# One chunk's state exchange of an mLSTM and MoE kernel: the same product on GpSimd, both states in one bank

## The chip, the cores and the metric

The kernel runs on one core of a Trainium2 chip. The metric is the device time of one execution in microseconds (us). The core has a matmul engine (TensorE, PE in the profile, with its weight loads as PEld), VectorE (DVE), ScalarE (ACT), GpSimd (POOL) and a queue for transfers (SyncE, SP). The engines run side by side and wait for each other by semaphores. PSUM, in which matmuls leave their results, has eight banks.

## The reference

Three stages follow one another. The first is a recurrent attention over 2 batches, 8 heads, 768 steps and 40 columns a head, with a decaying state `C` for each head:

```
for t in range(S):
    m_new  = maximum(f_gate[t] + m, i_gate[t])
    C      = exp(f_gate[t] + m - m_new) * C + exp(i_gate[t] - m_new) * outer(v[t], k[t])
    n      = exp(f_gate[t] + m - m_new) * n + exp(i_gate[t] - m_new) * k[t]
    y[t]   = sigmoid(o_gate[t]) * (C @ q[t]) / maximum(abs(n @ q[t]), 1)
x = y as 1536 tokens x 320
x = (h - tanh(h)) @ w_out,        h = x @ w_in      # layer 1, 2048 columns of h
x = (h * tanh(softplus(h))) @ w_out, h = x @ w_in   # layer 2, weights of its own
```

## The kernel before

The attention is computed in 6 chunks of 128 steps (c = 0 to 5). A tile is one chunk of one batch, 128 tokens with all 8 heads; the 12 tiles are numbered j = 2c + b, so that both batches of a chunk follow each other. Inside a tile, `sc` (L406) holds the scores of its steps among each other, `Dm` the weights from the gates, with a causal mask laid over it on GpSimd (L383); L410 multiplies both in place in `Dm`. `it` (L417) is what the state `C` of all chunks before gives, `pv` (L430) what the tile's own steps give. The sum is normed (L434 to L444: `hv`, `den`, `xo`) and, as the tokens `xo`, transposed on TensorE (`xt`, L296) into `xT` for layer 1. `xT` is kept as a rounded part, written by ScalarE (L298), and a low part that VectorE subtracts (L302, L304), because matmuls take a rounded 32-bit form (fp32r) and products are split into a high and a low part.

At the end of a tile the state is carried on. This is the exchange. `dl` (L171, called from L393) copies the last column of `Dm` into a small tile, `wv` (L394) multiplies the values of the tile by it, 8 small matmuls (`states`, L322; the trace counts each of such 32-bit matmuls as two) make of `wv` and the keys what the tile adds to the state, in a bank `st` of PSUM. Then `C` is multiplied by a decay `dec` of the chunk and `st` is added. For chunks 2 and later this is done for both batches at once, after the first batch's tile: 16 matmuls into one bank, one decay pass over `C` of both batches (L476), two sums (L479), all on VectorE. For chunk 1 each batch does it by itself, with 8 matmuls and a bank of its own, four decay passes on GpSimd in all (L459) and four sums on VectorE (L461). Chunk 0 copies.

Layer 1 runs in blocks of two tiles, 256 tokens. Its 16 slices of 128 columns go in pairs: h (L606, 8 matmuls a slice), then the function of h in steps on ScalarE and VectorE (L628 to L637), then its rounded part `gh` on ScalarE (L617) and its low part `gl` on GpSimd (L618), then `acc` (L669 to L671). The slices of a block are begun while the next tiles' attention runs, so TensorE has work of both. Weights come raw in a packed form and are unpacked in passes on VectorE and ScalarE (L204, L212, L216, L219, L222). Layer 2 begins at about 257 us and has blocks of 512 tokens.

The order of instructions on each engine is decided when the kernel is built, by a scheduler that works from its own estimate of how long each operation takes, under the data's dependences and a few edges `after(...)` written into the code. Work further down the program can therefore change places when an operation changes. From the second block on, the attention's PSUM tiles (`xt`, `st`, `nb`, `sc`, `it`, `pv`) share three banks in turn, so each of them waits until the one three before it is read. `nb` (L371) makes the gate terms of a half of `Dm`, which ScalarE reads through its exponential (L375); only chunks 0 to 2 have it.

For tile 2 (`j == NP`) an edge makes the copy `dl` wait for `rests[1]`, the `gl` of layer 1's second step, so that the copy comes behind that `gl` on GpSimd.

Of the kernel before, what the change touches and what calls it, by code (L numbers as in the profile page):

```python
# [12 lines left out]
ALU = mybir.AluOpType  # L13
# [12 lines left out]
def kernel(  # L26
# [11 lines left out]
    nc = tc.nc  # L38
    B, P, _, HG, S = qk.shape
    H, L = 2 * HG, 128  # L40
# [3 lines left out]
    D = DM // H  # L44
    NF, _, WC = w1.shape
    D1 = D + 1
# [17 lines left out]
    def cut(sizes, p0=0):  # L64
        r = []
        for n in sizes:
            r.append(list(range(p0, p0 + n)))
            p0 += n
        return r

    blocks1 = cut(BLOCKS)
    flat = cut([n for s in SUPER for n in s])
# [53 lines left out]
    dec = once.tile([P, B, HG, NCH], F32, name="dec")  # L126
# [4 lines left out]
    last, chain, fill, mark, second = [], [], [], [], []  # L131

    texp, tbl, dls, squared = [], [], [], []
# [14 lines left out]
    def after(x):  # L148
        e = ExitStack()
        for i in x:  # L150
            e.enter_context(tc.issue_after(i.ins))
        return e
# [12 lines left out]
    def copy_r(eng, o, x):  # L165
        if eng == 0:
            nc.scalar.activation(out=o, in_=x, func=AF.Copy)
        elif eng == 1:
            nc.vector.tensor_copy(o, x)
        else:  # L170
            nc.gpsimd.tensor_scalar(o, in0=x, scalar1=1.0, scalar2=0.0, op0=ALU.mult, op1=ALU.add)  # L171
# [103 lines left out]
    def at_ps(shape, name):  # L275
        p, tag = at_pools[0]
        if len(at_pools) > 1:
            at_pools.append(at_pools.pop(0))
        return p.tile(shape, F32, tag=tag, name=name)
# [37 lines left out]
    def states(st, k, wv, first):  # L317
        with in_turn(first=first) as turn:
            for g in range(HG):
                for r in range(2):  # L320
                    h = HG * r + g
                    turn(lambda: nc.tensor.matmul(  # L322
                        st[HP * r:HP * r + D, g, :], lhsT=k[:, h, :], rhs=wv[:, h, :], start=True, stop=True
                    ))
        return turned[-1:]
# [5 lines left out]
    def attention(j):  # L331
        b, c = order[j]
# [16 lines left out]
        Dm = att.pop(("D", j)) if c >= RC else ap_.tile([P, H, L], F32, tag="D", name="Dm", bufs=2)  # L349
        for hf in range(2):  # L350
            if c < RC:
                nb = at_ps([P, HG, L], "nb")
                flat = nb.rearrange("p g s -> p (g s)")
            if c < EC:
                bh = b * H + HG * hf
                nc.tensor.matmul(
                    flat, lhsT=na[c], rhs=sel[:, bh:bh + HG].rearrange("p (g o) -> p g o", o=1).to_broadcast([P, HG, L]),
# [30 lines left out]
        C = Cst[b]  # L388
        if c + 1 < NCH:
            wv = ap_.tile([P, H, D1], F32, tag="wv", name="wv", bufs=2)  # L390
            dl = ap_.tile([P, H, 1], F32, tag="dl", name="dl")
            with after([rests[1]] if j == NP else []):
                copy_r(2, dl, Dm[:, :, L - 1:L])  # L393
            dls[:] = [nc.gpsimd.tensor_tensor(wv, in0=v, in1=dl.to_broadcast([P, H, D1]), op=ALU.mult)]  # L394
            if c > 1:
                news.append((k, wv))
        scs = [at_ps([P, HG, L], "sc") for _ in range(2)]
        held = []
# [15 lines left out]
        if c > 0:  # L414
            it = at_ps([P, HG, 2, D1], "it")
            for g in range(HG):
# [7 lines left out]
                in1=u.to_broadcast([P, 2, HG, D1]), op=ALU.mult,  # L424
# [10 lines left out]
        else:  # L435
# [9 lines left out]
            x, in0=x, scalar=1 / WS, in1=den.to_broadcast([P, H, D]), op0=ALU.mult, op1=ALU.mult  # L445
# [3 lines left out]
        copy_r(0, xo[:, j, DM:3 * P], xo[:, j, 2 * P:DM])  # L449
        yield "x"  # L450
        if c + 1 < NCH:
            if c < 2:
                st = at_ps([P, HG, D1], "st")
                states(st, k, wv, chain[:1])
                for r in range(2):
                    sl = slice(HP * r, HP * r + D)
                    if c:
                        dc = dec[sl, b, :, c:c + 1].to_broadcast([D, HG, D1])
                        nc.gpsimd.tensor_tensor(C[sl, :, r, :], in0=C[sl, :, r, :], in1=dc, op=ALU.mult)  # L459
                        with after(chain[2:]):  # L460
                            nc.vector.tensor_tensor(C[sl, :, r, :], in0=C[sl, :, r, :], in1=st[sl], op=ALU.add)  # L461
                        continue
                    with after(cvd):
                        copy_r(0, C[sl, :, r, :], st[sl])
                return
            if b:
                return
            st = at_ps([P, B, HG, D1], "st")
            done = []
            for bb in range(B):  # L470
                done = states(st[:, bb], *news[bb], done or chain[:1])
            news.clear()
            flat = Call.rearrange("p b g r d -> p (b g) (r d)")
            dc = dec[:, :, :, c:c + 1].rearrange("p b g o -> p (b g) o")
            with after(chain[2:]):
                nc.vector.tensor_tensor(flat, in0=flat, in1=dc.to_broadcast([P, B * HG, 2 * D1]), op=ALU.mult)  # L476
            for r in range(2):
                sl = slice(HP * r, HP * r + D)
                nc.vector.tensor_tensor(Call[sl, :, :, r, :], in0=Call[sl, :, :, r, :], in1=st[sl], op=ALU.add)  # L479
# [223 lines left out]
    def program():  # L703
# [60 lines left out]
        session(0, 1)  # L764

        ga, gb = (attention(j) for j in blk[0, 0])

        def go(g, n=1):
# [42 lines left out]
        def attend():  # L811
            for k in range(1, NB):
                js = blk[0, k]
                gens, ready = [(n, attention(j)) for n, j in enumerate(js)], []
                if k < NB - 1:
                    new_xT(0, k)
                loads_to(js[0] + 1)
                if k >= RC:
                    loads_to(js[-1] + 1, "D")
                alone = 0  # L820
                while gens:
                    for n, g in list(gens[:1 if alone > 0 else 2]):
                        alone -= 1
                        loads_to(js[n] + 2)
                        if n in ready and k < NB - 1:
                            transpose_x(0, k, n)()
                            yield
                        x = next(g, 0)
                        if x == 0:
                            gens.remove((n, g))  # L830
                        elif x == "x":
                            ready.append(n)
                            if k >= RC - 1 and n == 0:
                                loads_to(js[n] + B + 1, "D")
                        yield
            left.close()
            late["x"] = pool(left, "lateX", 1, reuse_waits="tile")
            late["A"] = pool(left, "lateA", 2, reuse_waits="tile")
            yield from trans(0, NB - 1)
# [168 lines left out]
```

## Time and profile before

| what | value |
|---|---|
| median of 3 runs | 445.47 us (444.94 to 446.33) |
| the profiled execution's own time | 445.67 us |
| its span | 444.0 us |
| TensorE busy | 435.1 us (98%), granted clock 9 (of 9) in all 40 slices |
| VectorE busy | 298.7 us (67%) |
| ScalarE busy | 290.1 us (65%) |
| GpSimd busy | 100.9 us (23%) |
| chain that ended last, by engine | TensorE 73%, VectorE 12%, ScalarE 10%, GpSimd 1% |

The span runs from the first to the last instruction; 1.67 us of the execution's time lie around it. Times in the profile are microseconds from the span's start unless marked ns. A row of a timeline gives the start, the busy time of a run of like instructions, engine, line and operation, output and input tiles, the partitions and columns of one, the count, and in brackets how long the engine stood before it and what it waited for. Since matmuls overlap, the busy time of a row of TensorE is longer than what it holds the engine; the starts tell more.

### The profile page before, as it was taken

What the parts mean: (1) busy time and instruction counts of PE and PEld (TensorE: products, weight loads), DVE (VectorE), ACT (ScalarE), POOL (GpSimd) and SP (SyncE); (2) the same over time, 40 slices, a digit from 0 to 9 for tenths busy, and PEclk for the clock granted to TensorE, in tenths of its full rate; (3) what the DMA queues carried; (4) which work ended last, traced back from release to release, by engine and by line L of the source; (5) the groups of instructions that cost most, each with busy time, mean ns of one, the idle gap of its engine ahead of it and who ended that gap; (6) DMA issues with size and microseconds to landing.
All of it is one profiled execution on the core that took longest, in us unless ns stands there. A gap on an engine that the chain in (4) does not pass through costs nothing.

```text
span 444.0 us, 7980 instructions
## 1 busy us (share of the span) xinstructions
PE 435.1 (98%) x3108; PEld 397.7 (90%) x3108; DVE 298.7 (67%) x515; ACT 290.1 (65%) x555; POOL 100.9 (23%) x105
## 2 busy tenths in 40 slices
PE   9999989999999999999999999999999999999996
PEld 5657979999899998999999999999999889999996
DVE  7897999869989896678999969898323211211121
ACT  7688988687886968889889877666333322333321
POOL 2107436343543323244332340000000000000000
PEclk9999999999999999999999999999999999999999
DMA  8977527636344110001122120562010000100001
GB/s 244 378 278 257 163 75 269 185 100 183 127 147 121 66 67 2 0 1 66 65 68 66 65 66 0 196 195 68 0 61 0 1 0 1 56 4 0 1 0 59
DMA packets 28700, 41.13 MB, mean 93 GB/s; under 512 B 1352, under 2 KB 22984, under 8 KB 28664
## 3 DMA queue, kind: packets, MB, share of 16 engines
q1 hardware_dynamic: 28664, 40.64, 28.0%
q8 instruction: 24, 0.39, 0.4%
q14 instruction: 12, 0.10, 0.1%
HBM read 38.55 MB, written 2.02 MB: 91 GB/s over the span
## 4 chain that ended last, share of the span: by engine, by line
PE 73%; DVE 12%; ACT 10%; issue 3%; POOL 1%; DVEq 0%; ACTq 0%
PE h L606 34%; PE acc L670 11%; PE acc L671 11%; PE acc L669 11%; PE pv L430 2%; ACT Dm L379 2%; DVE g L633 1%; ACT raw L212 1%; ACT u L628 1%; ACT t L629 1%; PE sc L406 1%; ACT w L219 1%; PE xt L296 1%; PE w_ps L710 1%; DVE xo L444 1%
## 5 line engine op out<-in xcount | busy, mean ns | idle before, releaser
L606 PE MATMUL h<-xT,w 128*128 128x256 f32 (+1 forms) x1152 | 205.7, 321 | 0.7 <-DVE xT L302 0.3
L606 PEld LDWEIGHTS h<-xT,w 128*128 128x128 f32 x1152 | 167.6, 188 | 17.1 <-DVE xT L302 1.0
L669 PE MATMUL acc<-w,gh 128*128 128x320 f32 x384 | 119.4, 312 | 0.9 <-ACT gh L617 0.9
L670 PE MATMUL acc<-w,gh 128*128 128x320 f32 x384 | 118.6, 310 | 0.0
L671 PE MATMUL acc<-w,gl 128*128 128x320 f32 x384 | 113.9, 310 | 0.0
L618 POOL TENSOR_TENSOR gl<-g,gh 128x512 fp32r<-128x512 f32 x48 | 65.6, 1367 | 133.8 <-ACT gh L617 128.5
L650 DVE TENSOR_TENSOR gl<-g,gh 128x512 fp32r<-128x512 f32 x48 | 33.2, 691 | 89.3 <-ACT g L649 89.1
L648 ACT ACTIVATE gh<-h 128x512 fp32r<-128x512 f32 x48 | 28.7, 598 | 80.8 <-PE h L606 80.7
L669 PEld LDWEIGHTS acc<-w,gh 128*128 128x128 f32 x384 | 72.2, 188 | 3.7 <-ACT gh L617 1.2
L670 PEld LDWEIGHTS acc<-w,gh 128*128 128x128 f32 x384 | 72.2, 188 | 2.7 <-issue 0.4
L671 PEld LDWEIGHTS acc<-w,gl 128*128 128x128 f32 x384 | 70.3, 188 | 0.1
L637 DVE COPY_PREDICATED g<-u,t 128x512 f32<-128x512 uint32 x48 | 37.7, 785 | 12.9 <-ACT u L635 12.9
L617 ACT ACTIVATE gh<-g 128x512 fp32r<-128x512 f32 x48 | 30.4, 633 | 22.3 <-DVE g L637 18.6
L635 ACT ACTIVATE u<-u,bias 128x512 f32<-128x512 f32 x48 | 35.0, 728 | 4.4 <-DVE g L633 4.4
L633 DVE TENSOR_TENSOR g<-u,h 128x512 f32<-128x512 f32 x48 | 32.5, 676 | 6.2 <-ACT u L630 5.9
L222 DVE TENSOR_TENSOR w<-raw,w 128x704 fp32r<-128x704 f32 x32 | 34.8, 1090 | 1.2 <-ACT w L219 1.0
L219 ACT ACTIVATE w<-raw 128x704 fp32r<-128x704 f32 x32 | 27.4, 858 | 12.1 <-DVE raw L216 12.1
L634 DVE TENSOR_TENSOR t<-h,t 128x512 f32<-128x512 f32 x48 | 32.8, 683 | 0.0
L216 DVE SCALAR_TENSOR_TENSOR raw<-raw 128x704 uint32<-128x704 uint32 x32 | 30.0, 939 | 2.2 <-ACT raw L212 1.6
L630 ACT ACTIVATE u<-u 128x512 f32<-128x512 f32 x48 | 30.5, 639 | 0.0
L629 ACT ACTIVATE t<-h 128x512 f32<-128x512 f32 x48 | 28.6, 595 | 0.0
L649 ACT ACTIVATE g<-h 128x512 f32<-128x512 f32 x48 | 28.6, 595 | 0.0
(109 smaller groups left out, 438.4 us busy)
## 6 DMA issues: line engine op xcount, KB each, us to landing
raw<-in_w_dram SPq DMA_DIRECT2D x32, 704.0 KB
qk_t<-in_qk_dram SPq DMA_DIRECT2D x12, 512.0 KB
kv_t<-in_kv_dram SPq DMA_DIRECT2D x12, 324.0 KB
Dm<-nd SPq DMA_DIRECT2D x6, 512.0 KB
out_dram<-xo SPq DMA_DIRECT2D x12, 160.0 KB
xo<-in_og_dram SPq DMA_DIRECT2D x2, 800.0 KB
xo<-in_og_dram SPq DMA_DIRECT2D x1, 320.0 KB
sd<-nr SPq DMA_DIRECT2D x8, 4.0 KB
```

The costliest lines, as they stand in the source:

```text
L222: lows[layer, f] = eng.tensor_tensor(w[:, WC:WT], in0=zf, in1=wf[:, 0:WC], op=ALU.subtract)
L606: y = nc.tensor.matmul(t[:, k * nt:(k + 1) * nt], lhsT=w[:, o:o + P], rhs=x[:, kk, :], start=(n == 0), stop=(n == len(pairs) - 1),)
L618: rests[i] = nc.gpsimd.tensor_tensor(gl, in0=g, in1=gh.bitcast(F32), op=ALU.subtract)
L629: nc.scalar.activation(out=t, in_=h, func=AF.Tanh)
L633: mark[:] = [nc.vector.tensor_tensor(g, in0=u, in1=h, op=ALU.mult)]
L634: nc.vector.tensor_tensor(t, in0=h, in1=t, op=ALU.subtract)
L635: relus[i] = nc.scalar.activation(out=u, in_=u, func=AF.Relu, bias=bias[:, 0:1])
L637: chosen[i] = nc.vector.copy_predicated(out=g, mask=u.bitcast(U32), data=t)
L650: mark.append(nc.vector.tensor_tensor(gl, in0=g, in1=gh.bitcast(F32), op=ALU.subtract))
L669: turn(lambda: nc.tensor.matmul(a, lhsT=gh[:, sl], rhs=wh, start=(f in ends_), stop=False))
L670: turn(lambda: nc.tensor.matmul(a, lhsT=gh[:, sl], rhs=wl, start=False, stop=False))
L671: turn(lambda: nc.tensor.matmul(a, lhsT=gl[:, sl], rhs=wh, start=False, stop=end))
```

## The change

Two things change. For tile 2 the edge to `rests[1]` is now on the product `wv` alone, and no longer on the copy `dl` before it. And chunk 1 carries its state as later chunks do: the matmuls of both batches go into one bank after the first batch's tile, one decay pass goes over `C` of both batches, and two sums follow. For chunk 1 that pass is on GpSimd and has no edge to the transposes, where for later chunks it stays on VectorE. Computed is the same.

```diff
--- before.py
+++ after.py
@@ -389,10 +389,10 @@
         if c + 1 < NCH:
             wv = ap_.tile([P, H, D1], F32, tag="wv", name="wv", bufs=2)
             dl = ap_.tile([P, H, 1], F32, tag="dl", name="dl")
+            copy_r(2, dl, Dm[:, :, L - 1:L])
             with after([rests[1]] if j == NP else []):
-                copy_r(2, dl, Dm[:, :, L - 1:L])
-            dls[:] = [nc.gpsimd.tensor_tensor(wv, in0=v, in1=dl.to_broadcast([P, H, D1]), op=ALU.mult)]
-            if c > 1:
+                dls[:] = [nc.gpsimd.tensor_tensor(wv, in0=v, in1=dl.to_broadcast([P, H, D1]), op=ALU.mult)]
+            if c:
                 news.append((k, wv))
         scs = [at_ps([P, HG, L], "sc") for _ in range(2)]
         held = []
@@ -449,17 +449,11 @@
         copy_r(0, xo[:, j, DM:3 * P], xo[:, j, 2 * P:DM])
         yield "x"
         if c + 1 < NCH:
-            if c < 2:
+            if c < 1:
                 st = at_ps([P, HG, D1], "st")
                 states(st, k, wv, chain[:1])
                 for r in range(2):
                     sl = slice(HP * r, HP * r + D)
-                    if c:
-                        dc = dec[sl, b, :, c:c + 1].to_broadcast([D, HG, D1])
-                        nc.gpsimd.tensor_tensor(C[sl, :, r, :], in0=C[sl, :, r, :], in1=dc, op=ALU.mult)
-                        with after(chain[2:]):
-                            nc.vector.tensor_tensor(C[sl, :, r, :], in0=C[sl, :, r, :], in1=st[sl], op=ALU.add)
-                        continue
                     with after(cvd):
                         copy_r(0, C[sl, :, r, :], st[sl])
                 return
@@ -472,8 +466,10 @@
             news.clear()
             flat = Call.rearrange("p b g r d -> p (b g) (r d)")
             dc = dec[:, :, :, c:c + 1].rearrange("p b g o -> p (b g) o")
-            with after(chain[2:]):
-                nc.vector.tensor_tensor(flat, in0=flat, in1=dc.to_broadcast([P, B * HG, 2 * D1]), op=ALU.mult)
+            with after(chain[2:] if c > 1 else []):
+                (nc.vector if c > 1 else nc.gpsimd).tensor_tensor(
+                    flat, in0=flat, in1=dc.to_broadcast([P, B * HG, 2 * D1]), op=ALU.mult
+                )
             for r in range(2):
                 sl = slice(HP * r, HP * r + D)
                 nc.vector.tensor_tensor(Call[sl, :, :, r, :], in0=Call[sl, :, :, r, :], in1=st[sl], op=ALU.add)
```

Line numbers after L461 shift: L470 of the changed kernel is the decay pass, L475 the two sums, L602 is h (before L606), L613 and L614 are `gh` and `gl` (L617, L618), L665 to L667 are acc (L669 to L671).

The scheduler's order around the change, on GpSimd, before: from the masks of the second chunk to the decay passes.

```order
L383 AFFINE_SELECT Dm<-Dm 128x512 x3
L618 TENSOR_TENSOR gl<-g,gh 128x512
L171 TENSOR_SCALAR dl<-Dm 128x8
L394 TENSOR_TENSOR wv<-kv_t,dl 128x328
L383 AFFINE_SELECT Dm<-Dm 128x512
L171 TENSOR_SCALAR dl<-Dm 128x8
L394 TENSOR_TENSOR wv<-kv_t,dl 128x328
L618 TENSOR_TENSOR gl<-g,gh 128x512
L459 TENSOR_TENSOR C<-C,dec 40x4x41 x4
```

And in the changed kernel:

```order
L383 AFFINE_SELECT Dm<-Dm 128x512 x3
L171 TENSOR_SCALAR dl<-Dm 128x8
L614 TENSOR_TENSOR gl<-g,gh 128x512
L394 TENSOR_TENSOR wv<-kv_t,dl 128x328
L383 AFFINE_SELECT Dm<-Dm 128x512
L171 TENSOR_SCALAR dl<-Dm 128x8
L394 TENSOR_TENSOR wv<-kv_t,dl 128x328
L614 TENSOR_TENSOR gl<-g,gh 128x512
L470 TENSOR_TENSOR C<-C,dec 128x656
L383 AFFINE_SELECT Dm<-Dm 128x512 x2
L614 TENSOR_TENSOR gl<-g,gh 128x512
```

The first `gl` and the copy have changed places, the four decay passes have become one, and two masks of the next chunk stand ahead of the next `gl`.

On TensorE, the states of chunk 1 and what follows, before (`sd_97` and `sd_98` are the two batches' selectors, so the `nb` are those of tiles 4 and 5):

```order
L296 MATMUL xt<-ident,xo 128x128 x3
L322 MATMUL st<-wv,kv_t 40x41 x8
L296 MATMUL xt<-ident,xo 128x128 x3
L322 MATMUL st<-wv,kv_t 40x41 x8
L606 MATMUL h<-xT,w 128x256 x6
L371 MATMUL nb<-md,sd_97 128x512
L606 MATMUL h<-xT,w 128x256 x3
L371 MATMUL nb<-md,sd_98 128x512
L606 MATMUL h<-xT,w 128x256 x26
```

And in the changed kernel:

```order
L296 MATMUL xt<-ident,xo 128x128 x3
L322 MATMUL st<-wv,kv_t 40x41 x16
L296 MATMUL xt<-ident,xo 128x128 x3
L371 MATMUL nb<-md,sd_97 128x512
L602 MATMUL h<-xT,w 128x256 x6
L371 MATMUL nb<-md,sd_98 128x512
L371 MATMUL nb<-md,sd_97 128x512
L602 MATMUL h<-xT,w 128x256 x3
L371 MATMUL nb<-md,sd_98 128x512
L602 MATMUL h<-xT,w 128x256 x11
L401 LDWEIGHTS const-bfloat16-1.0
L401 MATMUL sc<-const-bfloat16-1.0 128x1
```

All 16 state matmuls stand ahead of the second tile's transposes, and all four `nb` are within the next ten matmuls, where two of them stood behind 26 h matmuls. The scores' first matmul (L401) also stands earlier.

Further on, 8 h matmuls stand between the scores (L406) of tiles 4 and 5, where there were 16.

On TensorE again, the acc matmuls late in layer 1, before (the fourth row is the first acc of a new `gh`):

```order
L669 MATMUL acc<-w,gh 128x320
L670 MATMUL acc<-w,gh 128x320
L671 MATMUL acc<-w,gl 128x320
L669 MATMUL acc<-w,gh 128x320
L670 MATMUL acc<-w,gh 128x320
L669 MATMUL acc<-w,gh 128x320
L670 MATMUL acc<-w,gh 128x320
L606 MATMUL h<-xT,w 128x256 x4
L671 MATMUL acc<-w,gl 128x320 x2
```

And in the changed kernel:

```order
L667 MATMUL acc<-w,gl 128x320
L665 MATMUL acc<-w,gh 128x320
L666 MATMUL acc<-w,gh 128x320
L667 MATMUL acc<-w,gl 128x320
L602 MATMUL h<-xT,w 128x256 x16
L665 MATMUL acc<-w,gh 128x320
L666 MATMUL acc<-w,gh 128x320
L665 MATMUL acc<-w,gh 128x320
L666 MATMUL acc<-w,gh 128x320
L602 MATMUL h<-xT,w 128x256 x6
```

Now 16 h matmuls stand directly ahead of the four acc, and six h behind them where there were four.

## Rows read from the trace of the kernel before

**Rows 1.** The page, part 1: busy us, share of the span, instructions, by engine.

```profile
PE 435.1 (98%) x3108; PEld 397.7 (90%) x3108; DVE 298.7 (67%) x515; ACT 290.1 (65%) x555; POOL 100.9 (23%) x105
```

**Rows 2.** TensorE's waits: us in total, times, longest.

```profile
PE st L322 <- DVE xT L304: 1.1, 1, 1.1
PE acc L669 <- ACT gh L617: 0.9, 1, 0.9
...
PE h L606 <- DVE xT L302: 0.3, 1, 0.3
...
PE h L606 <- DVE t L634: 0.2, 1, 0.2
PE sc L406 <- ACT Dm L375: 0.2, 1, 0.2
```

**Rows 3.** Windows, 200 to 260 us: PE, PEld, DVE, ACT, POOL, clock, DMA.

```profile
200.00:260.00 60.00, 60.00 (x458) 59.64 (x457) 54.91 (x89) 52.70 (x98) 21.50 (x17) 1.00 0.22 72
```

**Rows 4.** TensorE's timeline, 44 to 60 us: start, us, instructions, idle before.

```profile
45.03 1.12 PE L417 MATMUL it<-C,qk_t 128*128 128x82 f32 x8 [0.20 <-DVE Dm L410]
...
54.85 0.51 PE L322 MATMUL st<-wv,kv_t 128*40 128x41 f32 x16
55.29 0.55 PE L296 MATMUL xt<-ident,xo 128*128 128x128 f32 x3
56.95 0.51 PE L322 MATMUL st<-wv,kv_t 128*40 128x41 f32 x16 [1.11 <-DVE xT L304]
...
58.55 0.62 PE L606 MATMUL h<-xT,w 128*128 128x256 f32 x3
```

**Rows 5.** VectorE's timeline, 36 to 62 us.

```profile
42.85 0.69 DVE L410 TENSOR_TENSOR Dm<-sc,Dm 128x512 f32<-128x512 f32 x1 [1.35 <-POOL dl L171]
...
49.76 0.50 DVE L434 TENSOR_TENSOR hv<-hv,pv 128x328 f32<-128x328 f32 x1 [0.27 <-PE pv L430]
50.29 0.62 DVE L439 TENSOR_SCALAR den<-hv 128x8 f32<-128x8 f32 x1
...
51.23 0.43 DVE L440 TENSOR_TENSOR den<-hv,den 128x8 f32<-128x8 f32 x1
...
53.14 0.45 DVE L439 TENSOR_SCALAR den<-hv 128x8 f32<-128x8 f32 x1
...
56.72 0.67 DVE L461 TENSOR_TENSOR C<-C,st 40x164 f32<-40x164 f32 x2
...
58.20 0.29 DVE L302 TENSOR_TENSOR xT<-xt,xT 64x128 fp32r<-64x128 f32 x1
...
61.56 2.13 DVE L216 SCALAR_TENSOR_TENSOR raw<-raw 128x704 uint32<-128x704 uint32 x2
```

**Rows 6.** GpSimd's timeline, 37 to 64 us.

```profile
41.09 1.56 POOL L618 TENSOR_TENSOR gl<-g,gh 128x512 fp32r<-128x512 f32 x1
...
49.61 1.28 POOL L618 TENSOR_TENSOR gl<-g,gh 128x512 fp32r<-128x512 f32 x1 [3.62 <-ACT gh L617]
50.84 2.72 POOL L459 TENSOR_TENSOR C<-C,dec 40x164 f32<-40x164 f32 x4
```

**Rows 7.** TensorE's timeline, 97 to 99 us.

```profile
97.61 0.60 PE L606 MATMUL h<-xT,w 128*128 128x256 f32 x3
98.40 0.83 PE L606 MATMUL h<-xT,w 128*128 128x256 f32 x5 [0.20 <-DVE t L634]
```

**Rows 8.** Single lines: ns of one at least, median, at most; first and last start.

```profile
L394 POOL TENSOR_TENSOR wv<-kv_t,dl x10: 735/736/1491, 9.3 to 123.4; 128x328 f32<-128x328 f32 x10
...
L618 POOL TENSOR_TENSOR gl<-g,gh x48: 1268/1297/1967, 33.5 to 264.3; 128x512 fp32r<-128x512 f32 x48
...
L479 DVE TENSOR_TENSOR C<-C,st x6: 479/490/500, 88.9 to 144.6; 40x328 f32<-40x328 f32 x6
...
L476 DVE TENSOR_TENSOR C<-C,dec x3: 831/831/836, 86.9 to 141.8; 128x656 f32<-128x656 f32 x3
...
L439 DVE TENSOR_SCALAR den<-hv x10: 149/171/1035, 50.3 to 165.2; 128x8 f32<-128x8 f32 x10
```

## The prediction, made before the result was known

> **What bounds the kernel now.** I read the page first. TensorE is busy for 435.1 of 444.0 us [rows 1]. So a gain can only come out of the 8.9 us in which TensorE stands. The list of TensorE's waits says where the rest is [rows 2]. The longest wait, 1.1 us, is in the stretch that is changed. The others shown are waits of 0.2 to 0.9 us, met once each. The windows say from where on nothing can be won: between 200 and 260 us TensorE is busy for 60.00 of 60 us at a granted clock of 1.00, the full 2.4 GHz [rows 3]. A change that leaves the number of matmuls as it is counts only before that.
>
> Then the timelines around the change. TensorE waits 0.20 us at 45.03 before `it`, which needs a bank that VectorE's L410 is still reading. It then waits 1.11 us at 56.95, where the second tile's state matmuls need the bank that VectorE's low part L304 reads [rows 4]. VectorE itself stood 1.35 us at 42.85 for the copy `dl` on GpSimd, and later it runs the low parts, four sums and a select in one chain [rows 5]. The copy stood behind 1.56 us of `gl` on GpSimd, and the four decay passes run from 50.84 to 53.56 [rows 6].
>
> **The change part by part.**
>
> *The wait moved from the copy to the exchange product.* `dl` reads a column of `Dm` that L410 overwrites, so VectorE had to wait for it. Now `gl` and the copy change places on GpSimd. The copy no longer waits for 1.56 us of `gl`, so the 1.35 us on VectorE go. The product `wv` still stands behind `gl` and is no later than before; its readers, the state matmuls, stand at 54.85 [rows 4]. For TensorE the earlier copy is worth the wait at 45.03. A printed wait understates the loss, since the pipeline restarts: at 97.61 three matmuls start, the next at 98.40; five last 0.83 and three 0.60, so one costs 0.115, and 0.79 − 3 × 0.115 = 0.44 is lost where 0.20 is printed [rows 7]. So 0.4 us is gained at 45. What remains of VectorE's 1.35 us isn't kept: at 49.76 VectorE waits 0.27 us for TensorE's pv [rows 5], so from there it is only as early as TensorE is. VectorE is what the gap at 56.95 ends on. There TensorE's lead counts only as far as VectorE is earlier too, by at least 0.27 us. I take −0.3, with bounds of 0 (the gap eats it all) and −0.4.
>
> *Both states in one bank, after tile 2.* Before, a tile's 8 state matmuls (16 in the trace), the transposes of tile 3, then the wait of 1.11 us, then the other 8. Now all 16 stand before the transposes of tile 3. A tile's state matmuls hold TensorE for 0.44 us (54.85 to 55.29) [rows 4], so 0.44 us of work moves ahead of the gap and fills that much. What waits for L304 now is the first `nb` matmul. Behind it VectorE runs two sums, a select, and then L302 of tile 3. A sum over twice the columns lasts 0.49 us [rows 8] where two small ones last 0.67 together [rows 5]. So 0.98 us stand where 0.67 stood, and L302 of tile 3, from 58.20 to 58.49 before, ends about 0.3 later, near 58.8. Three h matmuls wait for it. Before, they started at 58.55 with one `nb` done. Now they start near 58.85 with three done. An `nb` matmul holds TensorE for about 0.23 us (512 columns at twice the 0.115 us of 256), so 0.46 − 0.3 = 0.16, and I take −0.2. Bounds: the whole gap of 1.11 gone, and +0.5 where the longer chain of sums isn't covered at all (0.3, and a restart of 0.2 as above). The other two sums of 0.67, at 60.86 before, vanish from VectorE, where they were hidden: there are no TensorE waits there.
>
> *One decay pass on GpSimd in place of four.* No row has this shape there. From 128x328 in 0.736 us and 128x512 in 1.297 us [rows 8] the slope is 0.561/184 = 3.05 ns a column, so 128x656 is estimated at 1.297 + 144 × 0.00305 = 1.74 us, against 2.72 us for the four. Bounds: 0.83 us, the same shape on VectorE [rows 8], and 2.72. GpSimd is busy for 23% of the span [rows 1], so its own time is taken as free. What costs is VectorE's small operations beside it. L439 lasts 0.171 us as a rule but 0.62 at 50.29 and 0.45 at 53.14 [rows 5, 8], and these end where an instruction of GpSimd ends: 50.91 beside `gl`'s end of 50.89, and 53.59 beside 53.56 [rows 6]. There are three such rows in the stretch, with L440 at 51.23 (0.43, to 51.66), about 1.0 us lost together, all on the chain to the gap at 56.95. With one pass from 50.9 to about 52.6, L440 could stand until 52.6 in place of 51.66, and the row at 53.14 is then free: +0.97 − 0.28 = +0.7. If nothing is held, −1.0. I take +0.2, nearer to the upper end, since the row at 50.29 did stand to the end of what ran. The Trainium skill, page "SBUF — State Buffer", section "SBUF: two separate sides", says that the port pair that GpSimd and VectorE share is a lock held for a whole instruction, and that the loser blocks fully. The ends of the two rows agree with that. By that rule L440 stands to the end of the pass, which is rival 3.
>
> *The order behind.* The scheduler lays out everything after 57 us anew. The last two `nb` stand ahead of 26 h matmuls that they stood behind. TensorE's later waits are 0.2 (scores on Dm), 0.2 (h on t), 0.3 (h on L302) and 0.9 (acc on `gh`) [rows 2], 1.6 us printed, and with a restart of 0.2 each 2.4 us. The largest gets new cover: in the new order 16 h matmuls, 16 × 0.115 = 1.8 us, stand ahead of the four acc that waited, where other acc stood and four h matmuls came only after. But the same rows bring new tight places. The second scores now have 8 h matmuls between them and the first ones, 0.92 us, where there were 16. The transposes of tile 4 come 12 acc earlier. I count half of it as kept: −1.2, with bounds of 0 and −2.4.
>
> Sum: −0.3 − 0.2 + 0.2 − 1.2 = −1.5 on the profiled execution of 445.67, which is 444.17. The median of the three runs, 445.47, lies 0.2 below that execution, so the prediction is 444.0. The 1.67 us around the span are not touched.
>
> **The rivals.**
> 1. *All later waits go.* Then they count fully: 445.67 − 0.3 − 0.2 + 0.2 − 2.4 − 0.2 = 442.8. For it: each of the four is met once and is short, so a little lead removes it. Against it: the new order has tight places of its own, named above.
> 2. *The lead is given back.* TensorE waits elsewhere for as much: 445.67 − 0.3 − 0.2 + 0.2 − 0.2 = 445.2, no change. For it: ScalarE and VectorE, which release these waits, do the same work as before less 0.36 us (1.34 for four sums before, 0.98 now).
> 3. *The one pass holds VectorE to its end.* At the estimated 1.74 us the term is +0.7 in place of +0.2, so 444.5. At 2.72 us L440 stands until 53.6: 53.6 − 51.66 − 0.28 = +1.7, so 445.5. Half way it is 445.0, no change. For it: the ends of the two small rows. Against it: where TensorE's 0.44 us of new work lies in the gap, a VectorE that is late by less is covered.
> 4. *Slower: VectorE late at the second scores.* The third bank comes free only when L410 of tile 4 is done with the first scores. Ahead of that L410 VectorE has six conversion passes; a pair lasts 2.13 us [rows 5]. TensorE is back after 0.92 us, and L410 lasts 0.69 [rows 5], so 0.23 us of slack are left. If two passes of that chain (2.13 us) come late, TensorE loses 2.13 − 0.23 + 0.2 = 2.1, and with nothing of the later waits won: 445.67 − 0.3 − 0.2 + 0.2 + 2.1 − 0.2 = 447.3. For it: the tight place is new, and VectorE still has all its other work of the stretch. Against it: with the other two sums gone VectorE has 0.67 us less to do before. It is slower than measurement can tell from VectorE being about 1.7 us late at that L410.
>
> **How the numbers follow.** The forecast has 0.52, with its own range of 442.9 to 445.0; rival 1 has 0.14, rival 2 0.14, rival 3 0.06, rival 4 0.14. A difference under 0.3%, 1.34 us, can't be told from none: faster is below 444.13, slower above 446.81. The forecast lies just below the first bound, so of its 0.52 about 0.31 are faster and 0.21 no change. Faster: 0.31 + 0.14 = 0.45. No change: 0.21 + 0.14 + 0.06 = 0.41. Slower: 0.14. The range goes from 442.4, a little below rival 1, to 447.0, which takes in the smaller part of rival 4.
>
> **What the changed profile would show.** VectorE's first L410 of tile 2 begins near 41.5 with no wait for L171, and TensorE's `it` at 45 has no gap. The wait of `st` for L304 is replaced by one of `nb` for L304 of some 0.7 us and one of h for L302 of 0.3 to 0.6. GpSimd has one row of 128x656 of about 1.7 us in place of four, and VectorE's L440 beside it ends when it ends. The acc behind the 16 h near 170 us has no wait. I am wrong if VectorE's rows between 50 and 55 are longer in sum by over 1 us, if the second scores of tile 5 show a wait of over 1 us, or if the sum of TensorE's waits between 60 and 175 us stays at 1.6 us or grows.

## The result, and the profile after

The changed kernel is slower: 449.47 us median of 12 executions against 445.96 us (444.64 to 446.33). One of the twelve, 478.69 us at a mean clock of 0.844, was disturbed and is left out of the ratio; the others took 447.06 to 450.17 us. The ratio is 1.0063, interval 1.0046 to 1.0079. In a later comparison on another chip it was 1.0090 (1.0077 to 1.0104). Forecast was 444.0, a gain of 0.3%.

The profiled execution took 447.06 us, span 445.3, at a granted clock of 1.00 throughout. The first line of its page stands beside [rows 1]: TensorE does the same work in the same time, and the span is 1.3 us longer. 0.39 us of that is older than the change: the `nb` row that starts at 37.57 before starts at 37.96 here, and up to there both kernels do the same. In the other profiles it starts between 37.49 and 38.53, so times of two profiles are best counted from that row.

```profile
PE 435.1 (98%) x3108; PEld 397.9 (89%) x3108; DVE 300.2 (67%) x513; ACT 291.4 (65%) x555; POOL 97.4 (22%) x102
```

TensorE's waits in it (us in total, times, longest), beside [rows 2]:

```profile
PE h L602 <- DVE xT L302: 2.3, 2, 2.0
PE xt L296 <- DVE xo L444: 1.3, 3, 0.9
PE nb L371 <- ACT xT L298: 1.0, 1, 1.0
```

Of the five waits of [rows 2] only that of h for the low part L302 is left, and it has grown from 0.3 us to 2.3 us in two places; the 0.9 us for `gh` is gone. New are two waits of the transposes for the gating L444 (the third, at 18 us, was there before) and one of 1.0 us for a rounded copy. The timeline of TensorE says where:

```profile
45.15 1.12 PE L417 MATMUL it<-C,qk_t 128*128 128x82 f32 x8
...
54.91 0.81 PE L322 MATMUL st<-wv,kv_t 128*40 128x41 f32 x32
55.66 0.55 PE L296 MATMUL xt<-ident,xo 128*128 128x128 f32 x3
57.18 0.47 PE L371 MATMUL nb<-md,sd 128*128 128x512 f32 x1 [0.97 <-ACT xT L298]
...
59.16 0.62 PE L602 MATMUL h<-xT,w 128*128 128x256 f32 x3 [0.27 <-DVE xT L302]
...
84.47 0.41 PE L296 MATMUL xt<-ident,xo 128*128 128x128 f32 x2 [0.89 <-DVE xo L444]
...
86.69 0.41 PE L296 MATMUL xt<-ident,xo 128*128 128x128 f32 x2 [0.23 <-DVE xo L444]
...
119.45 0.62 PE L602 MATMUL h<-xT,w 128*128 128x256 f32 x3 [1.98 <-DVE xT L302]
```

The first five rows answer to [rows 4]. `it` has no wait, the two states run as one piece, and the gap of 1.11 us has become 0.97 ahead of the first `nb` and 0.27 ahead of the h matmuls. The last three are new: 0.89 and 0.23 us at 84 to 87, 1.98 us at 119. Up to 60 us the kernel does nearly what was forecast; the loss lies in stretches that no line of the diff touches.

VectorE and GpSimd in the changed stretch, beside [rows 5, 6]:

```profile
41.97 0.69 DVE L410 TENSOR_TENSOR Dm<-sc,Dm 128x512 f32<-128x512 f32 x1
...
50.84 1.26 DVE L440 TENSOR_TENSOR den<-hv,den 128x8 f32<-128x8 f32 x1
...
56.34 0.29 DVE L302 TENSOR_TENSOR xT<-xt,xT 64x128 fp32r<-64x128 f32 x1
...
58.81 0.30 DVE L302 TENSOR_TENSOR xT<-xt,xT 64x128 fp32r<-64x128 f32 x1
```

```profile
41.58 0.35 POOL L171 TENSOR_SCALAR dl<-Dm 128x8 f32<-128x8 f32 x1
...
50.79 1.29 POOL L470 TENSOR_TENSOR C<-C,dec 128x656 f32<-128x656 f32 x1 [0.35 <-PE it L417]
```

L410 starts at 41.97 without a wait, the copy is done ahead of `gl`, and the pass over 128x656 took 1.29 us. L440 beside it lasted 1.26 us, to 52.10, where the pass ends at 52.08. L302 of tile 2 starts at 56.34; before, it was 0.27 us earlier:

```profile
56.07 0.29 DVE L302 TENSOR_TENSOR xT<-xt,xT 64x128 fp32r<-64x128 f32 x1
```

Then VectorE ahead of the long wait at 119:

```profile
114.36 0.42 DVE L304 TENSOR_TENSOR xT<-xt,xT 128x256 fp32r<-128x256 f32 x1
114.70 1.33 DVE L204 TENSOR_SCALAR raw<-raw 128x704 uint32<-128x704 uint32 x1
115.95 0.83 DVE L470 TENSOR_TENSOR C<-C,dec 128x656 f32<-128x656 f32 x1
116.71 1.16 DVE L633 COPY_PREDICATED g<-u,t 128x512 f32<-128x512 uint32 x1
117.76 1.31 DVE L216 SCALAR_TENSOR_TENSOR raw<-raw 128x704 uint32<-128x704 uint32 x1
119.10 0.29 DVE L302 TENSOR_TENSOR xT<-xt,xT 64x128 fp32r<-64x128 f32 x1
```

Between the low part of tile 6 (114.36) and that of tile 7 (119.10) four passes stand in the new order: an unpacking pass, the decay pass of chunk 3, a select, another unpacking pass, 4.6 us in all. TensorE ran out of other work at 117.5.

The wait at 87 us has two sizes. It is 0.23 us here and 1.37 us in a second profile of the same kernel (run 12), without any edit. What differs is VectorE's L440, the small operation ahead of the gating of tile 5. Here:

```profile
84.89 0.15 DVE L440 TENSOR_TENSOR den<-hv,den 128x8 f32<-128x8 f32 x1
```

And in run 12:

```profile
84.39 1.27 DVE L440 TENSOR_TENSOR den<-hv,den 128x8 f32<-128x8 f32 x1
```

In both a `gl` of GpSimd starts 0.1 us ahead of it (84.77 and 84.29). In run 12 L440 ends when that `gl` does (85.66 and 85.63), here it doesn't wait for it. Why it comes out one way or the other is not shown.

**The clock.** The profiled execution is one of three of the twelve with a mean granted clock of 1.000; the eight others in the ratio had 0.994 to 0.996. One such execution was profiled later (449.25 us, mean 0.996). Its windows around the wait (columns as in [rows 3]):

```profile
118.00:120.00 2.00, 0.10 (x1) 0.00 (x0) 1.97 (x3) 2.00 (x8) 1.17 (x2) 1.00 0.00 0
120.00:122.00 2.00, 1.92 (x17) 1.78 (x19) 1.78 (x5) 2.00 (x5) 1.83 (x4) 0.70 0.03 8
122.00:124.00 2.00, 2.00 (x13) 1.78 (x12) 1.21 (x2) 0.60 (x1) 1.92 (x4) 0.50 0.00 0
124.00:126.00 2.00, 2.00 (x18) 1.96 (x18) 1.89 (x3) 0.90 (x2) 0.34 (x1) 0.95 0.00 0
126.00:128.00 2.00, 2.00 (x25) 1.75 (x24) 1.06 (x2) 2.00 (x5) 0.00 (x0) 1.00 0.56 175
```

TensorE was busy 0.10 of 2 us between 118 and 120; then its clock was 0.70, 0.50 (the lower of its two levels, 1.2 GHz) and 0.95, then 1.00 again. That costs 2 × (0.30 + 0.50 + 0.05) = 1.7 us of work at full clock. By the starts of the same matmuls it is 1.5 us: this execution is 0.63 us behind the first one at the end of the wait (120.08 against 119.45) and 2.18 us behind at the next L401 (124.91 against 122.73). The kernel before isn't free of such falls, but they are smaller: 0.998 to 1.000 in all but one of its executions in the same comparison as run 1. Nor does the mean give the time by itself: one execution of run 5 had 0.994 and took 444.14 us, as little as any of that run.

### The profile page after: what moved, and what is told of

It is laid out like the page before. It is cut to its first block, busy times and chain, and to the rows that moved or that the text cites. A ratio compares the mean times of both kernels' runs of the same rounds, so it can differ in the third digit from the quotient of the medians.

```text
span 445.3 us, 7981 instructions
## 1 busy us (share of the span) xinstructions
PE 435.1 (98%) x3108; PEld 397.9 (89%) x3108; DVE 300.2 (67%) x513; ACT 291.4 (65%) x555; POOL 97.4 (22%) x102
## 4 chain that ended last, share of the span: by engine, by line
PE 83%; DVE 12%; ACT 3%; issue 2%; ACTq 0%; DVEq 0%
PE h L602 38%; PE acc L667 12%; PE acc L665 12%; PE acc L666 12%; PE sc L406 3%; PE pv L430 2%; DVE g L629 1%; DVE t L630 1%; PE w_ps L706 1%; PE xt L296 1%; DVE raw L216 1%; DVE xo L444 1%; PE it L417 1%; DVE g L633 1%; DVE raw L204 1%
## 5 line engine op out<-in xcount | busy, mean ns | idle before, releaser
L602 PE MATMUL h<-xT,w 128*128 128x256 f32 (+1 forms) x1152 | 204.7, 321 | 2.5 <-DVE xT L302 2.3
L602 PEld LDWEIGHTS h<-xT,w 128*128 128x128 f32 x1152 | 167.7, 188 | 18.2 <-DVE xT L302 3.1
L665 PE MATMUL acc<-w,gh 128*128 128x320 f32 x384 | 119.2, 312 | 0.0
L667 PE MATMUL acc<-w,gl 128*128 128x320 f32 x384 | 114.1, 311 | 0.0
L614 POOL TENSOR_TENSOR gl<-g,gh 128x512 fp32r<-128x512 f32 x48 | 63.9, 1331 | 133.5 <-ACT gh L613 130.9
L665 PEld LDWEIGHTS acc<-w,gh 128*128 128x128 f32 x384 | 72.1, 188 | 2.9 <-ACT u L626 0.4
L667 PEld LDWEIGHTS acc<-w,gl 128*128 128x128 f32 x384 | 70.2, 188 | 0.3
L633 DVE COPY_PREDICATED g<-u,t 128x512 f32<-128x512 uint32 x48 | 39.4, 820 | 11.9 <-ACT u L631 11.8
L613 ACT ACTIVATE gh<-g 128x512 fp32r<-128x512 f32 x48 | 30.3, 632 | 17.6 <-DVE g L633 14.0
L629 DVE TENSOR_TENSOR g<-u,h 128x512 f32<-128x512 f32 x48 | 32.5, 678 | 9.5 <-ACT u L626 9.1
L631 ACT ACTIVATE u<-u,bias 128x512 f32<-128x512 f32 x48 | 34.7, 724 | 4.9 <-DVE g L629 4.6
L222 DVE TENSOR_TENSOR w<-raw,w 128x704 fp32r<-128x704 f32 x32 | 33.9, 1062 | 3.0 <-ACT w L219 2.8
L630 DVE TENSOR_TENSOR t<-h,t 128x512 f32<-128x512 f32 x48 | 32.8, 683 | 0.0
L624 ACT ACTIVATE u<-h 128x512 f32<-128x512 f32 x48 | 28.2, 588 | 3.5 <-PE h L602 3.4
```

Source lines behind the costliest of these rows:

```text
L222: lows[layer, f] = eng.tensor_tensor(w[:, WC:WT], in0=zf, in1=wf[:, 0:WC], op=ALU.subtract)
L602: y = nc.tensor.matmul(t[:, k * nt:(k + 1) * nt], lhsT=w[:, o:o + P], rhs=x[:, kk, :], start=(n == 0), stop=(n == len(pairs) - 1),)
L614: rests[i] = nc.gpsimd.tensor_tensor(gl, in0=g, in1=gh.bitcast(F32), op=ALU.subtract)
L629: mark[:] = [nc.vector.tensor_tensor(g, in0=u, in1=h, op=ALU.mult)]
L630: nc.vector.tensor_tensor(t, in0=h, in1=t, op=ALU.subtract)
L631: relus[i] = nc.scalar.activation(out=u, in_=u, func=AF.Relu, bias=bias[:, 0:1])
```

## The experiments

Most runs hold the engines to an order by edges without waiting, put in behind the program from a table of instruction names, so that one thing can be changed while all else stays (shortened):

```
for a, b in zip(row, row[1:]):
    tc.add_manual_dep(known[b], a, DependencyInfo(NoSync, DATA), reason="pin")
```

Theory O is that the new order causes the loss, rival L that the changed instructions do. All ratios are to the kernel before on the same chip.

**1. The changed instructions in the old order.** The edit: the changed kernel, with the table of the kernel before, in which only the 8 state matmuls of tile 3, the one pass, the two sums and the copy stand in new places.

> The changed kernel with every engine held to the order of the kernel before; only the copy dl, the 16 state matmuls, the one decay pass and the two sums stand where the change puts them. Theory O (the scheduler's new order behind 60 us costs the time, in waits near 84 and 119 us, and the changed instructions themselves don't): 0.4 to 1.0 us under the kernel before, about 445.0 to 445.6, and the wait of 0.9 us at 171 us is there as before. Rival L (the changed instructions cost it: the one pass on GpSimd holds VectorE, or the two wide sums are late): 1 to 3 us over the kernel before, with longer waits between 50 and 60 us.

446.58 us, ratio 1.0014 (1.0004 to 1.0024): 0.6 us slower, neither theory's number, but a quarter of the loss or less. TensorE's rows in it:

```profile
57.48 0.97 PE L602 MATMUL h<-xT,w 128*128 128x256 f32 x6 [0.69 <-ACT xT L298]
...
59.70 0.63 PE L602 MATMUL h<-xT,w 128*128 128x256 f32 x3 [1.02 <-DVE xT L302]
```

Here the wide sums hold up the low part of tile 3: 1.02 us at 59.70. At 119 the wait is 0.33 us, as before the change (0.34).

**2. The old instructions in the new order.** The edit: the kernel before with the changed kernel's table behind 60 us, its own instructions in their own places.

> The kernel before (two banks, four decay passes, the copy behind gl), held from 60 us on to the order that the changed kernel has there. Theory O: the waits near 84 (0.9 and 0.2 us) and 119 us (2.0 us) come with it and the one at 171 us goes; 1 to 4 us over the kernel before, like the changed kernel. Rival L: no slower than the kernel before, 445 to 446.

449.54 us, ratio 1.0093 (1.0074 to 1.0113), with these rows:

```profile
68.64 1.16 PE L406 MATMUL sc<-qk_t 64*128 64x128 f32 x16 [0.96 <-DVE Dm L410]
...
85.48 0.41 PE L296 MATMUL xt<-ident,xo 128*128 128x128 f32 x2 [1.00 <-DVE xo L444]
...
120.38 0.69 PE L606 MATMUL h<-xT,w 128*128 128x256 f32 x3 [1.98 <-DVE xT L302]
```

The waits at 85 and 120 us are those of the changed kernel. The order alone brings the whole loss; of theory L no more is left than the 0.14% of run 1. A wait of 0.96 us of the second scores for L410 is there too, in the place of rival 4, which the changed kernel does not have.

**3 and 4. One and two moves in the new order.** In the lists, + marks where an instruction stands now and - where it stood.

```diff
+ L302, L304 of tile 7
  L470 decay pass; L633 select; L216 unpacking pass
- L302, L304 of tile 7
(4 also, on VectorE)
  L441 of tile 4
+ L444 of tile 4
  L630; L439 and L443 of tile 5; L633
- L444 of tile 4
```

> The changed kernel in its own order, but for one move on VectorE: the low parts of tile 7 (L302, L304) stand ahead of a decay pass, a select and an unpacking pass that they stood behind. Theory O: TensorE's wait of 2.0 us at 119 us goes, 2 us less than the changed kernel at full clock, about 445 to 446. Should the granted clock's mean of 0.994 to 0.996 in nine of the changed kernel's twelve executions hang on that wait, it is 1.000 here in all, and the gain 3 us or more over the median. Rival L: the wait moves elsewhere, the time stays at 447 or more.

> As the run before it, and beside that the gating product of tile 4 (L444) moved ahead of four passes on VectorE, so that the transposes at 84 us find it done. Theory O: another 0.9 us less, 444 to 445, under the kernel before. Rival L: no less than the changed kernel's 447.

Run 3: 447.11 us, ratio 1.0031 (1.0019 to 1.0043). Run 4: 446.48 us, 1.0014 (0.9997 to 1.0030), no difference from the kernel before that is clear. The wait at 119 is gone in both, and with it the fall of the clock: 0.999 to 1.000 in all six executions of run 3 and in nine of eleven of run 4 (two at 0.996). But not all that was expected came. In run 3:

```profile
87.43 0.41 PE L296 MATMUL xt<-ident,xo 128*128 128x128 f32 x2 [1.39 <-DVE xo L444]
...
122.24 0.16 PE L401 MATMUL sc<-const-bfloat16-1.0 128*128 128x1 bf16 x1 [0.92 <-DVE C L475]
```

The wait of 1.39 us at 87 doesn't come from the move: run 12, which has none, shows it too (1.37), and in both L440 is long (1.26 and 1.27 us). New is the one of 0.92 us at 122 for the sums of chunk 3 (L475), which the moved low parts pushed back. In run 4 the wait at 84 passed on to the next acc, which waits for its `gh` (1.55 us at 85.66 in its timeline).

**5. The copy alone, and 10. the states alone.** Each is half of the diff. The order of all engines but GpSimd is, instruction for instruction, that of the kernel before in run 5 and that of the changed kernel in run 10.

```diff
+ copy_r(2, dl, Dm[:, :, L - 1:L])
  with after([rests[1]] if j == NP else []):
-     copy_r(2, dl, Dm[:, :, L - 1:L])
      dls[:] = [nc.gpsimd.tensor_tensor(wv, ...)]
```

> The kernel before with the first part of the change alone: the copy dl no longer waits for gl. The order of the other engines stays that of the kernel before. Theory O: TensorE's wait at 45 us goes (0.4 us with its restart), but VectorE's chain to the wait at 57 us starts behind TensorE's pv and is earlier by 0.3 us at most, so 0 to 0.4 us under the kernel before, and nothing behind 60 us changes. Rival: the lead is given back whole at 57 us, the time is that of the kernel before.

> The changed kernel with its first part undone: the copy dl waits for gl again, only the states are in one bank with one pass on GpSimd. The order of the other engines is that of the changed kernel. Theory O: all of the loss is this part's, since it is what makes the scheduler lay out the order anew: the waits near 84 and 119 us are there, the time is that of the changed kernel or up to 0.7 us more (what the copy alone gave), 449 to 451. Rival: the two parts only lose together, and this run is within 1 us of the kernel before.

Run 5: 444.48 us, ratio 0.9986 (0.9975 to 0.9998). Run 10: 450.90 us, ratio 1.0123 (1.0102 to 1.0144). The two parts pull in opposite directions. In run 5 `it` has no wait, and the gap near 57 us is smaller:

```profile
45.24 1.12 PE L417 MATMUL it<-C,qk_t 128*128 128x82 f32 x8
...
56.85 0.51 PE L322 MATMUL st<-wv,kv_t 128*40 128x41 f32 x16 [0.86 <-DVE xT L304]
```

0.25 of its 1.11 us are gone, and TensorE gets there earlier. Counted from the `nb` row near 38 us (38.04 here, 37.57 before), `it` starts 0.26 us sooner and the second state 0.57 us. So the lead at 45 us reaches the state matmuls, and is worth more there than the forecast's 0.3 us; the interval of the ratio, 0.1 to 1.1 us, holds both.

The profile of run 5 gains another 0.7 us near 170 us, and that isn't shown to be the copy's. Near 153 us an unpacking pass of VectorE stands beside a `gl` of GpSimd. In the kernel before:

```profile
153.42 1.65 DVE L204 TENSOR_SCALAR raw<-raw 128x704 uint32<-128x704 uint32 x1
```

```profile
153.39 1.29 POOL L618 TENSOR_TENSOR gl<-g,gh 128x512 fp32r<-128x512 f32 x1
```

And in run 5:

```profile
153.37 0.52 DVE L204 TENSOR_SCALAR raw<-raw 128x704 uint32<-128x704 uint32 x1
```

```profile
153.34 1.70 POOL L618 TENSOR_TENSOR gl<-g,gh 128x512 fp32r<-128x512 f32 x1
```

The order is the same and so is the distance of the two starts, 0.03 us, yet once the one is long and once the other. Behind the short pass ScalarE's `gh` starts 1.19 us sooner (169.26 against 170.45), and TensorE's wait for it is 0.25 us in place of 0.95. The pass is long in the profiles of the kernel before and of runs 1 and 7, and short (0.51 to 0.54 us) in all others. Each profile is one execution; whether an edit favours one outcome is not shown.

**6. The low parts of tile 3 first (in the old order of run 1).**

```diff
+ L302, L304 of tile 3
  L475 x2 sums; L633 select
- L302, L304 of tile 3
```

> The changed instructions in the old order (the run with every engine held to it), with one move on VectorE: the low parts of tile 3 (L302, L304) stand ahead of the two wide sums and the select. Theory: that run lost 1.0 us at 59.7 because the wide sums (0.99 us) stand ahead of L302; here that wait goes and the time is 0.8 to 1.1 us under that run, at or under the kernel before. Rival: the sums, now later, hold the bank that the next nb needs, and the wait moves there: no gain.

446.50 us, ratio 1.0041 (1.0017 to 1.0064): no gain on run 1. The wait at 59.7 went, and TensorE was 1.9 us earlier at the scores of tile 4 than in run 1 (0.64 us of that from ahead of 38 us), to wait there:

```profile
57.88 0.52 PE L602 MATMUL h<-xT,w 128*128 128x256 f32 x3
...
67.89 1.16 PE L406 MATMUL sc<-qk_t 64*128 64x128 f32 x16 [2.34 <-ACT Dm L375]
```

```profile
59.60 0.64 ACT L613 ACTIVATE gh<-g 128x512 fp32r<-128x512 f32 x1 [2.81 <-DVE g L633]
...
67.17 0.67 ACT L375 ACTIVATE Dm<-nb 128x512 f32<-128x512 f32 x1
```

The bank for the scores comes free with the third exponential (67.17). ScalarE works up to it without a wait from the `gh` at 59.60 on, and that `gh` waited 2.81 us (1.99 in run 1) for the select L633, which the moved low parts pushed back. The rival was right in kind, though the bank is another one: what TensorE wins at 60 us is given back at 68.

**7. Five moves in the old order.** The six acc around tile 3's transposes, tile 2's and 3's low parts ahead of L629 and L630, tile 3's rounded copy ahead of L631, tile 7's low parts ahead of L222, `gh` ahead of L298 near 170 us.

> The changed instructions in the old order with five moves: low parts of tiles 2 and 3 early on VectorE, six acc around the transposes of tile 3, tile 3's rounded copy ahead of a relu on ScalarE, tile 7's low parts ahead of an unpacking pass, and gh ahead of a transpose's copy near 170 us. Theory: the waits near 57, 60 and 118 us shrink by 0.6, 1.0 and 0.4 us and the one at 171 by 0.4: 2 us or more under the run in the old order, 444 to 444.6, and under the kernel before. Rival: each wait moves to the next operation on its engine, and the sum of TensorE's waits stays within 0.5 us.

446.48 us, ratio 1.0033 (1.0017 to 1.0050). The rival: the scores of tile 4 wait 1.7 us, and h waits three times for L630, now late.

**8. The decay pass on VectorE (in the old order).**

```diff
-                (nc.vector if c > 1 else nc.gpsimd).tensor_tensor(
+                nc.vector.tensor_tensor(
```

> The changed instructions in the old order, with the decay pass of chunk 1 on VectorE too, behind the gating product of tile 2, in place of GpSimd. If the pass on GpSimd holds VectorE to its end (VectorE's L440 lasted 1.26 us beside it in the changed kernel, 0.16 us alone), L440 is back at 0.2 us, the pass takes 0.83 us of VectorE in its place, and the low parts come 0.2 to 0.3 us earlier; within 0.4 us of the run in the old order. Rival: L440 was long for another reason and stays long; then this run is 0.8 us slower than that one.

444.99 us, ratio 0.9988 (0.9979 to 0.9998), faster than run 1 by 0.26%, about 1.2 us, where 0.4 at most was expected. VectorE's rows:

```profile
51.23 0.16 DVE L440 TENSOR_TENSOR den<-hv,den 128x8 f32<-128x8 f32 x1
...
52.35 0.83 DVE L470 TENSOR_TENSOR C<-C,dec 128x656 f32<-128x656 f32 x1
```

L440 is back at 0.16 us, the pass takes 0.83. That the pass on GpSimd held VectorE to its end is shown. Between the two profiles about 0.5 us of the gain is made here: the h matmuls behind L302 start at 59.05 where run 1 has 59.70, and 0.16 us of that is from ahead of 38 us. Another 0.7 us is the wait for `gh` near 170 us, 0.27 us where run 1 has 0.95. It goes back to the unpacking pass near 154 us, 0.52 us here and 1.64 us in run 1, that is to the two outcomes told under run 5; how much of the difference of the medians is that, is not shown.

**9. More moves in the new order.** Those of run 4, chunk 3's sums behind their pass, L222 behind the gating of tile 5, tile 3's low parts ahead of the sums, six acc around its transposes, its rounded copy ahead of L631.

> The changed kernel in its own order with the two moves that took out the waits at 84 and 119 us, and more of the kind: the sums of chunk 3 directly behind their decay pass, an unpacking pass that stood ahead of the gating of tiles 4 and 5 behind it, tile 3's low parts ahead of the wide sums, six acc around tile 3's transposes, and tile 3's rounded copy ahead of a relu. Theory O (all of the loss is where single passes stand on VectorE and ScalarE): the waits left in the run with both moves, 1.2 and 0.4 us near 57 to 60, 1.5 us at 85.7 and 0.9 us at 122, shrink by 2 us or more, the time is 444 to 445, under the kernel before. Rival G (VectorE and ScalarE are full in these stretches, a pass moved ahead holds up another): the waits come back elsewhere, 446 to 447.

447.90 us, ratio 1.0066 (1.0047 to 1.0085): worse than run 4. VectorE and then the windows, in its profile:

```profile
61.25 2.44 DVE L216 SCALAR_TENSOR_TENSOR raw<-raw 128x704 uint32<-128x704 uint32 x2 [0.88 <-ACT raw L212]
65.39 2.51 DVE L222 TENSOR_TENSOR w<-raw,w 128x704 fp32r<-128x704 f32 x2 [1.70 <-ACT w L219]
67.93 0.69 DVE L410 TENSOR_TENSOR Dm<-sc,Dm 128x512 f32<-128x512 f32 x1
```

```profile
68.00:70.00 2.00, 1.32 (x14) 1.32 (x16) 2.00 (x4) 1.72 (x5) 0.00 (x0) 0.75 0.96 341
70.00:72.00 2.00, 2.00 (x13) 1.78 (x11) 2.00 (x5) 0.52 (x1) 0.00 (x0) 0.50 0.75 256
72.00:74.00 2.00, 2.00 (x18) 2.00 (x18) 2.00 (x5) 1.46 (x4) 0.55 (x1) 0.90 0.20 84
```

VectorE's unpacking passes waited for ScalarE's (0.88 and 1.70 us), L410 of tile 4 ended at 68.6, and the second scores waited 1.67 us for it. That is rival 4, in a kernel where it does happen; behind it the clock is at 0.75, 0.50 and 0.90, as behind the wait at 119.

**11. The copy and two moves, in the old order.** Edit to run 5: six acc stand around tile 3's transposes, ahead of the second state; L302 and L304 of tile 7 ahead of L222.

> The kernel before with the copy alone (the run that was faster), held to its order but for two moves: six acc stand around tile 3's transposes and ahead of the second tile's state matmuls, where TensorE waits 0.9 us, and tile 7's low parts stand ahead of an unpacking pass on VectorE, where it waits 0.3 us at 118 us. Theory: TensorE's work put into a wait is a gain where the waited-for operation isn't later for it, 0.5 to 1.2 us under the run with the copy alone, 443.3 to 444.0. Rival: the wait near 57 us ends on a chain that starts with TensorE's pv and the waits behind it take the lead back, as in the runs before: within 0.3 us of the run with the copy alone.

444.92 us on a chip where the kernel before took 446.14; ratio 0.9981 (0.9972 to 0.9990). By the ratios 0.2 us under run 5, not to be told from it, as the rival had it. The wait ahead of the second state is 0.82 us where run 5 had 0.86, though six acc (0.9 us) now stand between the transposes and it:

```profile
53.63 0.49 PE L296 MATMUL xt<-ident,xo 128*128 128x128 f32 x3
...
56.78 0.51 PE L322 MATMUL st<-wv,kv_t 128*40 128x41 f32 x16 [0.82 <-DVE xT L304]
```

The transposes of tile 2 are 0.95 us earlier (53.63 against 54.58), and the second state starts only 0.07 us sooner: it waits for VectorE's chain. Of the second move the 0.3 us at 118 went, and 0.6 us came at 126 (h for L634).

**12. The changed kernel again**, unedited, for the rows of the clock shown above.

> The changed kernel once more, for the rows of an execution at less than full clock. Theory: where the granted clock's mean is below 1.000, it falls behind the wait of 2.0 us at 119 us, to half for 2 to 4 us, which costs 1 to 2 us beside the wait itself; elsewhere it stays at 1.00. Rival: the low clock is spread over the span or sits at another place, and the wait has nothing to do with it.

450.16 us in four executions, 0.994 to 0.996 in all. The rows are as the theory had them: 1.00 in every other window asked for, 0.50 behind the wait. They also show the wait of 1.37 us at 87 us.

## Why the prediction was wrong

The step that failed is "The order behind", the −1.2 with bounds of 0 and −2.4. It counted the waits that the new order takes away and priced none of those that it makes. It named the place of one: "the transposes of tile 4 come 12 acc earlier". These 12 acc were the cover of VectorE's gating, and 0.89 + 0.23 us of waits stand there now (0.87 + 1.37 in run 12). The place of the larger one, 119 us, it didn't look at. The printed waits between 60 and 175 us are 3.1 us in the profiled execution (0.89, 0.23, 1.98) and 4.2 us in run 12, where the four of [rows 2] that lie there come to 1.6; the condition "stays at 1.6 us or grows" is met. The end of 0 for that term excluded a loss without a reason. Run 2 shows that the order by itself costs 0.93%, run 1 that the rest costs 0.14%.

Nor did it have the clock. [rows 3] show 1.00 and were read as a constant; a wait of 2 us costs 1.5 to 1.7 us again where the clock falls behind it. The span of run 12 is 2.2 us longer than that of the first profile (447.5 against 445.3): 1.5 us are the clock and 1.1 us the wait at 87 us, less 0.45 us by which it was ahead near 38 us. How the other executions divide is not shown: the eight below 1.000 took 447.8 to 450.2 us, and one at 1.000 took 448.10. Run 3 ties the fall to the wait at 119: with the wait gone the clock stayed.

The local steps, by their own terms:

- The copy, −0.3: right in kind, and too small. The wait at 45 went. The lead there, taken as 0.4, was 0.26 us, but 0.57 us arrived at the second state in run 5, beyond the bound of 0.4: VectorE's chain gained more than was counted. Run 5 measures the whole part at −0.6 (−1.1 to −0.1), in which the outcome near 153 us can have a share.
- Both states in one bank, −0.2: 0.44 us of work filled the gap, as forecast. The h matmuls start at 59.16, not 58.85, but 0.39 us of that is from ahead of the change. At 61.25 us 84 h matmuls and all four `nb` are issued; before, 84 h matmuls and two `nb` were at 60.65, which with the forecast's 0.23 us for each further `nb` is 61.11. Less the 0.39 us, the three local terms together are worth −0.25 by this estimate, where −0.3 was forecast. That is in part luck, for they don't add up singly: without the copy (run 10) the other two cost about 0.5 us at the same point, where the forecast has −0.2 + 0.2.
- The pass on GpSimd, +0.2: from L434 (49.82, before 49.76) to L302 of tile 2 (56.34, before 56.07) VectorE took 0.21 us longer, so the size holds. The estimate of 1.74 us for the pass was too long (1.29), and VectorE's L440 stood to its end, as rival 3 says. The rule of the Trainium skill cited for it, page "SBUF — State Buffer", section "SBUF: two separate sides", agrees with the two rows of the changed kernel (52.10 and 52.08) and with run 8.
- The acc behind the 16 h near 170 us has no wait, as forecast, but that its new cover did this is not shown. In the profile of the changed kernel the unpacking pass near 153 us is the short one (0.52 us), and run 5 with the old cover then waits 0.25 us. By that, 0.7 of the 0.95 us is luck.
- Rival 4 had the side, not the place. Its place is tight, as runs 2 and 9 show (0.96 and 1.67 us), but in the changed kernel L410 was in time, and the two places that weren't are of the same kind: an operand that VectorE finishes last, under less cover than before.

## What to carry to other kernels

Where a scheduler sets the order, a small edit is two changes: what the lines do, and a new order everywhere behind. Price them apart: hold the old order and test the lines, and read the new order for every matmul that comes earlier than it did and ask what used to cover its operand. Here, taking away one wait of TensorE mostly made another one elsewhere (runs 3, 4, 6 and 7). A profile is one execution: two of the same kernel differ by 1.1 us in one wait, so look at a second before a wait is put down to an edit. The part worth keeping here is the copy ahead of `gl` (ratio 0.9986, 0.9975 to 0.9998); the states in one bank aren't, as the order stands.

## What was not expected of the hardware

Behind a wait of 1.7 to 2.0 us TensorE's clock fell in four profiles (run 2 at 120, run 9 at 69, run 10 at 122 and run 12 at 120 us): each has a window of 2 us at 0.50 soon behind it, and in the window before and the one after between 0.67 and 0.98. It did not fall in three: the first profiled execution of the changed kernel with the same 1.98 us, run 6 with 2.34 us and run 7 with 1.73 us. So such a wait can bring the fall and need not; why it spares some stays open.

Where an operation of VectorE and one of GpSimd start within 0.12 us of each other, which one stands can differ from one execution to the next. L204 near 154 us lasted 0.51 to 0.54 us in eleven profiles and 1.64 or 1.65 us in three; L440 near 85 us lasted 0.15 us in two profiles of the new order (the first one and run 2) and 1.25 to 1.27 us in three (runs 3, 10 and 12). At TensorE the first is worth up to 0.7 us, the second 1.1 us.
